# Seeds and table copies of an S4D kernel generator moved in the planned order of a two-head kernel

## The chip, the cores and the metric

One core of a Trainium2 chip runs the whole kernel in one launch. The metric is the device time of that core in microseconds (us). The number to predict is the median of several runs of the changed kernel; the kernel before has a median of 586.85 us over 3 runs (586.58 to 588.71). A difference under 0.5% (2.9 us) is about what a measurement of this kernel can't tell from no change.

## The reference

Two heads work on inputs of 2048 positions and 512 channels, and their outputs stand side by side. Head A is a Fourier mix by dense matrices; head B is a long convolution whose kernel comes from a diagonal state-space model with 128 states per channel.

```
a = einsum("bsd,ed->bse", x, dft_hid_re);  b = einsum("bsd,ed->bse", x, dft_hid_im)
yA = einsum("ts,bse->bte", dft_seq_re, a) - einsum("ts,bse->bte", dft_seq_im, b)

A = -exp(log_A_real) + 1j * A_imag;  dt = exp(log_dt);  C = (C_real + 1j * C_imag) * dt[:, None]
P = exp((A * dt[:, None])[:, :, None] * pos[None, None, :])
K = 2.0 * einsum("dn,dnl->dl", C, P).real
yB = irfft(rfft(u, 2L) * rfft(K, 2L), 2L)[:, :, :L] + u * D_skip
out = concatenate([yA, yB], axis=-1)
```

## The kernel before, in words

**The plan.** Every piece of work is a Python generator that yields an engine, an assumed duration, and where it matters an urgency, and then records its instructions. `Plan.run` picks, of all pieces that wait, the one with the earliest start by the assumed durations; a tie is broken by the urgency (lower goes first), then by the number of the piece. So the assumed durations (`act`, `dve`, `load`, the numbers after `yield "pe"`) and the urgencies fix one order of instructions on each engine at build time. On the chip every engine takes its instructions in that order and waits on semaphores.

```
start = max(p[0], self.free.get(engine, 0.0))
...
return start, urgency[0]() if urgency and urgency[0] else p[1], p[2]
```

**Head A (`Fnet`).** There are 8 groups of 16 items and then 4 groups of 8. An item is a 128x512 block of the moving matrix: it is loaded (`raw`, L300, four buffers), split by ScalarE into `hi` (L212) and by VectorE into `lo` (L216) (three pairs of buffers, `DEPTH`), and used by 12 matmuls of 128x512 (L333): four column blocks by three products of high and low parts. The blocks of x (`x_hi`, `x_lo`, same lines) are split once, at the start. There are 1920 matmuls at L333. They are the filling between everything else on TensorE. A group ends in four evacuations `y` (L359).

**Head B (`Ssm`).** The 512 channels are cut into 16 units of 32. For each unit:
- `seed_args` makes angles on ScalarE (L620, four of L622), reduces them on VectorE (L624, L626, L628), and takes Abs, Exp and Sin on ScalarE (L630 to L638, with two ACT_TABLE_LOADs, in front of L632 and L634; for the first unit only the one in front of L634). From the fifth unit on its parameters come by a DMA first (`par`, L568, one buffer).
- `seeds` multiplies them (VectorE, `cs` L647) and copies each half with its sign (ScalarE, L652).
- `tables2` starts the table `t2` (64 powers; one buffer, `t2s`) with copies on ScalarE (L715, L718) and fills it by products (L577), additions (L586, L600, L606) on VectorE and squares (L593) on ScalarE. `tables1` does so for `t1` (32 powers, two buffers; its copy is L695).
- `taps` takes t1 and t2 on TensorE (L773, 128 small matmuls); only then is `t2` free for the next unit.

Two units make one `stage1_k` (L803). Beside it run the spectrum of u (L848, 8 times, at the start), 16 products of spectra (L929 on TensorE, then `uk` L941 on ScalarE, which frees the PSUM bank, then VectorE L944 to L957), their inverse (L964, joined to the next `taps` where one is left) and 8 last steps (L1011). All small TensorE work of head B shares two pairs of PSUM banks (`fs`).

## Time and profile before

| what | value |
|---|---|
| median of 3 runs | 586.85 us |
| the profiled execution, its own time | 587.23 us |
| its span, first to last instruction | 585.4 us |
| TensorE busy | 578.6 us (99%) |
| VectorE busy | 494.8 us (85%) |
| ScalarE busy | 381.4 us (65%) |

A matmul is pipelined: it shows 0.39 us, while the next one starts after 0.23 us. "Idle before" in a row is the time in which the engine had nothing to do in front of that instruction, with the one that ended the wait behind the arrow.

### The profile page before, as it was taken

What the parts mean: (1) busy time and instruction counts of PE and PEld (TensorE: products, weight loads), DVE (VectorE), ACT (ScalarE), POOL (GpSimd) and SP (SyncE); (2) the same over time, 40 slices, a digit from 0 to 9 for tenths busy, and PEclk for the clock granted to TensorE, in tenths of its full rate; (3) what the DMA queues carried; (4) which work ended last, traced back from release to release, by engine and by line L of the source; (5) the groups of instructions that cost most, each with busy time, mean ns of one, the idle gap of its engine ahead of it and who ended that gap; (6) DMA issues with size and microseconds to landing.
All of it is one profiled execution on the core that took longest, in us unless ns stands there. A gap on an engine that the chain in (4) does not pass through costs nothing.

```text
span 585.4 us, 14916 instructions
## 1 busy us (share of the span) xinstructions
PE 578.6 (99%) x5968; PEld 441.6 (75%) x5968; DVE 494.8 (85%) x883; ACT 381.4 (65%) x745; POOL 4.0 (1%) x12
## 2 busy tenths in 40 slices
PE   8999999999999999999999999999999999999997
PEld 7767677788777877787777778777877777777775
DVE  6986989999999999999999999999999984252620
ACT  4789894954775668677775777596756535354622
POOL 0000000000000000000000000000000000000000
PEclk9999999999999999999999999999999999999999
DMA  8999996473384276735987685458698945899684
GB/s 262 324 356 333 309 331 217 125 204 107 103 264 119 87 194 187 208 90 145 273 241 214 170 255 147 134 154 270 194 296 235 266 128 176 219 354 301 200 260 145
DMA packets 141238, 125.84 MB, mean 215 GB/s; under 512 B 46192, under 2 KB 106352, under 8 KB 140912
## 3 DMA queue, kind: packets, MB, share of 16 engines
q1 hardware_dynamic: 140880, 124.48, 70.1%
q8 instruction: 47, 0.77, 0.6%
q10 hardware_dynamic: 288, 0.39, 0.2%
q14 instruction: 23, 0.19, 0.1%
HBM read 82.12 MB, written 42.73 MB: 213 GB/s over the span
## 4 chain that ended last, share of the span: by engine, by line
PE 92%; ACT 3%; DMA 2%; DVE 1%; issue 1%; SPq 0%; DVEq 0%; ACTq 0%
PE acc L333 72%; PE f L773 5%; PE f L929 5%; PE f L964 3%; PE f L848 3%; PE f L1011 3%; PE f L803 2%; DMA par<-par_dram 1%; DMA raw<-in_sT 1%; ACT hi L212 1%; ACT L634 0%; DVE prod L577 0%; ACT seed L622 0%; ACT xk_sb L812 0%; ACT y L359 0%
## 5 line engine op out<-in xcount | busy, mean ns | idle before, releaser
L333 PE MATMUL acc<-hi,x_hi 128*128 128x512 f32 x640 | 257.0, 402 | 0.6 <-ACT x_hi L212 0.5
L333 PE MATMUL acc<-lo,x_hi 128*128 128x512 f32 x640 | 249.9, 390 | 0.0
L333 PE MATMUL acc<-hi,x_lo 128*128 128x512 f32 x640 | 249.5, 390 | 0.0
L577 DVE TENSOR_TENSOR prod<-t,cs 128x1024 f32<-128x1024 f32 (+4 forms) x192 | 163.9, 870 | 3.3 <-ACT t L715 1.3
L333 PEld LDWEIGHTS acc<-hi,x_hi 128*128 128x128 f32 x640 | 120.1, 188 | 48.0 <-issue 20.8
L216 DVE TENSOR_TENSOR lo<-raw,hi 128x512 fp32r<-128x512 f32 x160 | 109.9, 687 | 52.9 <-ACT hi L212 39.4
L212 ACT ACTIVATE hi<-raw 128x512 fp32r<-128x512 f32 x160 | 100.7, 630 | 80.5 <-PE acc L333 56.6
L333 PEld LDWEIGHTS acc<-hi,x_lo 128*128 128x128 f32 x640 | 120.3, 188 | 26.4 <-DVE x_lo L216 0.5
L333 PEld LDWEIGHTS acc<-lo,x_hi 128*128 128x128 f32 x640 | 120.2, 188 | 23.2 <-DVE lo L216 0.2
L586 DVE TENSOR_TENSOR t<-prod 128x512 f32<-128x512 f32 (+4 forms) x192 | 95.1, 514 | 1.1
L593 ACT ACTIVATE square<-t 128x256 f32<-128x256 f32 (+1 forms) x64 | 36.7, 573 | 26.3 <-DVE t L586 25.0
L941 ACT ACTIVATE uk<-f 128x1024 f32<-128x1024 f32 x32 | 31.6, 1015 | 5.5 <-PE f L929 4.8
L773 PEld LDWEIGHTS f<-t,t 128*32 128x32 f32 x2048 | 29.4, 110 | 7.5 <-issue 4.1
L359 ACT ACTIVATE y<-acc 128x512 f32<-128x512 f32 x47 | 27.8, 597 | 11.0 <-PE acc L333 10.8
L773 PE MATMUL f<-t,t 128*32 128x64 f32 x2048 | 32.1, 220 | 1.4 <-ACT uk L941 1.4
L929 PE MATMUL f<-xt,w 64*32 64x256 f32 x1024 | 31.3, 379 | 0.1
L944 DVE TENSOR_TENSOR z<-uk 128x512 f32<-128x512 f32 x32 | 22.0, 687 | 9.8 <-ACT uk L941 9.8
L929 PEld LDWEIGHTS f<-xt,w 64*32 64x32 f32 x1024 | 18.6, 106 | 10.8 <-issue 4.3
L606 DVE TENSOR_TENSOR t<-square 128x128 f32<-128x128 f32 (+1 forms) x64 | 24.8, 388 | 0.0
L979 ACT ACTIVATE z<-f 128x512 f32<-128x512 f32 x32 | 17.4, 597 | 11.1 <-PE f L773 7.2
L652 ACT ACTIVATE cs<-cs 128x352 f32<-128x352 f32 x32 | 15.8, 541 | 13.3 <-DVE cs L647 13.3
L600 DVE SCALAR_TENSOR_TENSOR t<-t 128x128 f32<-128x128 f32 (+2 forms) x48 | 22.4, 466 | 0.2
(81 smaller groups left out, 409.7 us busy)
## 6 DMA issues: line engine op xcount, KB each, us to landing
raw<-in_sT SPq DMA_DIRECT2D x127, 256.0 KB, 3.7
p<-y SPq DMA_DIRECT2D x32, 256.0 KB, 3.4
xt<-xu SPq DMA_DIRECT2D x32, 256.0 KB, 4.6
xk<-xk_sb SPq DMA_DIRECT2D x32, 256.0 KB, 4.0
xt<-xk SPq DMA_DIRECT2D x32, 256.0 KB, 5.1
zs<-z SPq DMA_DIRECT2D x32, 256.0 KB, 4.0
zl<-zs SPq DMA_DIRECT2D x16, 512.0 KB, 6.2
raw<-p SPq DMA_DIRECT2D x32, 256.0 KB, 4.2
```

The lines of the kernel that those rows point to most:

```text
L212: self.nc.scalar.activation(hi, src, AF.Copy)
L216: self.nc.vector.tensor_tensor(lo, src, hi.bitcast(F32), op=OP.subtract)
L333: nc.tensor.matmul(acc[d], l[:, cols], r, start=k == 0 and n == 0, stop=k == len(items) - 1 and n == 2)
L359: self.nc.scalar.activation(y, ps, AF.Copy, scale=-1.0 if g[2] == 1 else 1.0)
L577: self.nc.vector.tensor_tensor(p.rearrange("p k d c m -> p k (d c) m"), src.rearrange("p d c l -> p (d c) l")[:, None, :, rows].to_broadca ...
L586: self.nc.vector.tensor_tensor(dst[:, :, :, rows], p[:, 0], p[:, 1, :, ::-1], op=OP.add)
L593: self.nc.scalar.activation(sq, t[:, :, :, m // 2:m], AF.Square)
L600: self.nc.vector.scalar_tensor_tensor(t[:, :, 1, m:2 * m:2], t[:, :, 0, m // 2:m], 2.0, t[:, :, 1, m // 2:m], op0=OP.mult, op1=OP.mult)
L606: self.nc.vector.tensor_tensor(t[:, :, 0, m:2 * m:2], box[0][:, :, 0], box[0][:, :, 1], op=OP.subtract)
L773: nc.tensor.matmul(ps[32 * j:32 * j + 32, i], t1[:, d, c], t2[:, d, c], start=c == 0, stop=c == 1, tile_position=(0, 32 * j))
L929: nc.tensor.matmul(both[:, :, c], self.w2[rows, 2 * q + r, xx, 32 * c:32 * c + 32], xt[rows, r, xx], start=True, stop=True, tile_position= ...
L941: a.activation(uk[:, r].rearrange("p g n c d -> p g (n c d)"), p, AF.Copy)
```

## The change

No instruction is added or taken away; only urgencies and assumed durations change, so the order changes. The first unit's `seed_args` gets urgency -1 in place of 1, those of later units 1.8 in place of 1. `cs` (L647, L652) and the copies into the tables (L695, L715, L718) get the new urgency `soon` (-1). The assumed time of the first item's DMA, which ScalarE issues, falls from 0.78 + 3.3 us to 2.6 us; five assumed ScalarE durations rise; a joined `taps` is taken as 1.78 + 1.1 us in place of 1.78 + 0.87; the fetch of TensorE's next instructions is taken to be asked for 3.6 us behind the point at which it falls due, not 3.0.

```
-ASKED, APART_BY, COMES = 3.0, 4.3, 2.4
+ASKED, APART_BY, COMES = 3.6, 4.3, 2.4
+def soon():
+    return -1
...
             yield "act", 0.45
             self.nc.scalar.dma_start(raw, src)
-            yield "dma2", load(256)
+            yield "queue", 2.6
...
-        yield "act", act(2 * n) + 4 * act(0)
+        yield "act", 1.7
         a.activation(args[:, :, 0], par[:, 0:2], AF.Copy)
...
-        yield "act", act(n)
+        yield "act", 0.5
         a.activation(k, r, AF.Abs)
-        yield "act", act(n) + 1.3
+        yield "act", 0.5 + 1.3
         a.activation(e, e, AF.Exp, scale=-1.0)
...
-        yield "dve", dve(22 * CHUNK)
+        yield "dve", dve(22 * CHUNK), soon
         self.nc.vector.tensor_tensor(cs[:, :, :, :, 0], s[:, 1:3], s[:, 0:1].to_broadcast([128, 2, 11, CHUNK]),
...
-            yield "act", act(11 * CHUNK)
+            yield "act", 0.5, soon
             self.nc.scalar.activation(cs[:, n, :, :, 1], cs[:, n, :, :, 0], AF.Copy, scale=sign)
...
-        self.plan.spawn(self.seed_args(0, *args[0]), 1)
+        self.plan.spawn(self.seed_args(0, *args[0]), -1)
...
-                self.plan.spawn(self.seed_args(n + 1, *args[n + 1]), 1)
+                self.plan.spawn(self.seed_args(n + 1, *args[n + 1]), 1.8)
...
-            yield "act", act(2 * CHUNK)
+            yield "act", act(2 * CHUNK), soon
             a.activation(t[:, :, :, 1].rearrange("p d c -> p c d"), cs[:, :, 0, :, 0], AF.Copy)
...
-        yield "pe", 1.78 + (0.87 if other else 0), None, 322 if other else 257
+        yield "pe", 1.78 + (1.1 if other else 0), None, 322 if other else 257
```

The changed file is five lines longer ahead of all this work, so L212 of before is L217 of after, and so on.

**Place 1, the start on ScalarE.** The first item (`hi`, `raw`) and the first two blocks of x (`x_hi_146` in two pieces, then `x_hi_153`). Before:

```order
L296 DMA raw<-in_sT 128x512
L250 ACT_TABLE_LOAD
L250 ACTIVATE x_hi_146<-uk 128x128
L212 ACTIVATE hi<-raw 128x512
L212 ACTIVATE x_hi_153<-uk 128x512
L212 ACTIVATE x_hi_146<-uk 128x384
```

After:

```order
L301 DMA raw<-in_sT 128x512
L217 ACT_TABLE_LOAD
L217 ACTIVATE hi<-raw 128x512
L255 ACTIVATE x_hi_146<-uk 128x128
L217 ACTIVATE x_hi_146<-uk 128x384
L217 ACTIVATE x_hi_153<-uk 128x512
```

The first item's split moved ahead of the first piece of x, and the rest of x's first block ahead of its second block. VectorE's `lo` and `x_lo` follow in the same order.

**Place 2, the first unit's seeds on ScalarE** (`seed`, the lines from Abs to the last Sin; `zl` is an evacuation of the spectrum of u). Before:

```order
L630 ACTIVATE seed<-seed 128x352
L632 ACTIVATE seed<-seed 128x352
L634 ACT_TABLE_LOAD
L634 ACTIVATE seed<-seed 128x192
L212 ACTIVATE hi<-raw 128x512
L212 ACTIVATE x_hi_390<-uk 128x512
L858 ACTIVATE zl<-f_376 128x512 x2
L858 ACTIVATE zl<-f_377 128x512
L212 ACTIVATE x_hi_414<-uk 128x512
L212 ACTIVATE x_hi_431<-uk 128x512
L212 ACTIVATE hi<-raw 128x512
L212 ACTIVATE x_hi_442<-uk 128x512
```

After:

```order
L635 ACTIVATE seed<-seed 128x352
L637 ACTIVATE seed<-seed 128x352
L639 ACT_TABLE_LOAD
L639 ACTIVATE seed<-seed 128x192
L641 ACTIVATE seed<-seed 128x160
L643 ACTIVATE seed<-seed,halfpi 128x352
L217 ACTIVATE hi<-raw 128x512 x2
L217 ACTIVATE x_hi_381<-uk 128x512
L657 ACTIVATE cs<-cs 128x352 x2
L217 ACTIVATE hi<-raw 128x512
L720 ACTIVATE t_126<-cs 128x2x32
L723 ACTIVATE t_126<-cs 128x2x32 x2
```

Before, ten other instructions stand between the first Sin and the two last of the seeds; after, none, and the copies of `cs` and into the tables follow in the six rows behind them.

**Place 3, VectorE where the first tables begin** (`t_126` is t2, `t_625` and `t_484` are t1). Before:

```order
L626 TENSOR_TENSOR seed<-seed 128x352
L628 TENSOR_SCALAR seed<-seed 128x352
L216 TENSOR_TENSOR lo<-raw,hi 128x512 x3
L647 TENSOR_TENSOR cs<-seed 128x704
L577 TENSOR_TENSOR prod_638<-t_126,cs 128x128
L577 TENSOR_TENSOR prod<-t_625,cs 128x128
L586 TENSOR_TENSOR t_126<-prod_638 128x64
```

After:

```order
L629 TENSOR_SCALAR seed<-seed 128x352
L582 TENSOR_TENSOR prod_502<-t_126,cs 128x128
L631 TENSOR_TENSOR seed<-seed 128x352
L591 TENSOR_TENSOR t_126<-prod_502 128x64
L582 TENSOR_TENSOR prod<-t_484,cs 128x128
L633 TENSOR_SCALAR seed<-seed 128x352
L582 TENSOR_TENSOR prod_584<-t_126,cs 128x384
```

Before, the second unit's seed steps, three `lo` and the second unit's `cs` stand ahead of the first product; after, the first products stand between the second unit's seed steps, and no `lo` among them.

**Counted over the whole order.** TensorE has the same 137 runs of work in both orders, with 63 runs of L333 in each; what changes is how many matmuls of L333 lie in them. Ahead of the thirteenth `taps` stand 1338 matmuls of L333 before and 1266 after, and in both the same small pieces (12 of L773, 8 each of L848, L929 and L964, 6 of L803, 2 of L1011). Ahead of the fourteenth it is 1440 and 3 of L1011 before, 1395 and 4 after. Ahead of the first `taps` stand 273 and 7 runs of L848 before, 261 and 5 after. On VectorE, up to the last addition into the tables of the thirteenth unit, stand 687 instructions before and 677 after: six `lo` fewer, and one each fewer of L577 128x512, L577 128x256, L586 128x64x4 and L586 128x64x2. In VectorE's order 127 instructions before and 110 after read what the one right ahead of them wrote. On SyncE's queue the first three constants (0.25 MB) move from place 12 behind the loads of x to place 32, and w2 with ia (1 MB) from place 70 to place 40. On ScalarE, between the seventh unit's L620 and the first `uk` stand three `y`, three `hi` and two squares before, three `hi` and two squares after. ACT_TABLE_LOADs are 32 in both; GpSimd's order is the same.

## Rows read from the trace of the kernel before

**Rows 1.** The page, part 1: busy time of each engine

```profile
PE 578.6 (99%) x5968; PEld 441.6 (75%) x5968; DVE 494.8 (85%) x883; ACT 381.4 (65%) x745; POOL 4.0 (1%) x12
```

**Rows 2.** Waits of TensorE: line, waited for, total us, times, longest

```profile
PE f L773 <- ACT uk L941: 1.4, 1, 1.4
...
PE acc L333 <- ACT x_hi L212: 0.5, 1, 0.5
```

**Rows 3.** Timeline, 127 to 145 us, TensorE: start, us, instruction, count, idle

```profile
127.18 0.39 PE L333 MATMUL acc<-hi,x_hi 128*128 128x512 f32 x1
...
144.63 0.39 PE L333 MATMUL acc<-hi,x_lo 128*128 128x512 f32 x1
```

**Rows 4.** Timeline of the first 9 us, the three engines

```profile
3.56 0.31 ACT L250 ACTIVATE x_hi<-uk 128x128 fp32r<-128x128 f32 x1 [1.10 <-DMA uk<-in_x]
3.82 0.63 ACT L212 ACTIVATE hi<-raw 128x512 fp32r<-128x512 f32 x1
5.38 1.04 ACT L212 ACTIVATE x_hi<-uk 128x512 fp32r<-128x512 f32 x2 [0.93 <-DMA uk<-in_x]
6.04 1.16 DVE L216 TENSOR_TENSOR x_lo<-uk,x_hi 128x512 fp32r<-128x512 f32 x2 [0.87 <-ACT x_hi L212]
6.48 0.50 PE L333 MATMUL acc<-hi,x_hi 128*128 128x512 f32 x1 [0.48 <-ACT x_hi L212]
7.26 0.50 PE L333 MATMUL acc<-hi,x_lo 128*128 128x512 f32 x1
```

**Rows 5.** Timeline, 165 to 179 us: ScalarE, then TensorE

```profile
165.61 0.26 ACT L620 ACTIVATE seed<-par 128x64 f32<-128x64 f32 x1 [2.05 <-DMA par<-par_dram]
...
172.44 0.50 ACT L632 ACTIVATE seed<-seed 128x352 f32<-128x352 f32 x1
172.95 1.28 ACT L634 ACT_TABLE_LOAD   x1
174.25 0.37 ACT L634 ACTIVATE seed<-seed 128x192 f32<-128x192 f32 x1
...
175.74 1.00 ACT L941 ACTIVATE uk<-f 128x1024 f32<-128x1024 f32 x1
...
176.80 1.99 PE L773 MATMUL f<-t,t 128*32 128x64 f32 x128 [1.40 <-ACT uk L941]
```

**Rows 6.** Stretches: length, busy us of PE, PEld, DVE, ACT, POOL, clock, DMA

```profile
0.00:39.40 39.40, 37.72 (x160) 28.69 (x161) 33.53 (x74) 25.75 (x48) 0.20 (x4) 1.00 0.90 308
39.40:51.50 12.10, 12.10 (x53) 8.17 (x53) 4.77 (x9) 11.95 (x28) 0.00 (x0) 1.00 0.96 343
51.50:101.00 49.50, 49.50 (x332) 35.65 (x328) 47.36 (x89) 39.22 (x82) 0.00 (x0) 1.00 0.85 288
101.00:397.00 296.00, 294.53 (x3342) 228.71 (x3341) 290.83 (x519) 207.12 (x417) 3.11 (x6) 1.00 0.61 173
```

**Rows 7.** Timeline, 47 to 87 us, VectorE

```profile
47.46 0.69 DVE L216 TENSOR_TENSOR lo<-raw,hi 128x512 fp32r<-128x512 f32 x1 [4.42 <-ACT hi L212]
...
83.15 1.23 DVE L577 TENSOR_TENSOR prod<-t,cs 128x1024 f32<-128x1024 f32 x1
84.41 0.69 DVE L586 TENSOR_TENSOR t<-prod 128x512 f32<-128x512 f32 x1
86.80 0.69 DVE L216 TENSOR_TENSOR lo<-raw,hi 128x512 fp32r<-128x512 f32 x1 [1.69 <-ACT hi L212]
```

**Rows 8.** Timeline, 393 to 399 us: VectorE, then TensorE

```profile
393.28 1.22 DVE L577 TENSOR_TENSOR prod<-t,cs 128x1024 f32<-128x1024 f32 x1
394.41 0.69 DVE L216 TENSOR_TENSOR lo<-raw,hi 128x512 fp32r<-128x512 f32 x1
395.01 0.42 DVE L606 TENSOR_TENSOR t<-square 128x256 f32<-128x256 f32 x1
395.35 0.69 DVE L586 TENSOR_TENSOR t<-prod 128x512 f32<-128x512 f32 x1
...
397.23 1.99 PE L773 MATMUL f<-t,t 128*32 128x64 f32 x128
```

More of the change, by code (lines that the diff above doesn't have):

```diff
@@ L636, in seed_args @@
         a.activation(r[:, 6:11], r[:, 6:11], AF.Sin, scale=-TWO_PI)
-        yield "act", act(n)
+        yield "act", 0.5
         a.activation(k, k, AF.Sin, scale=-TWO_PI, bias=self.halfpi)
@@ L713, in tables2 @@
             cs, t = self.cs[n], self.t2
-            yield "act", act(2 * CHUNK)
+            yield "act", act(2 * CHUNK), soon
             a.activation(t[:, :, :, 1].rearrange("p d c -> p c d"), cs[:, :, 0, :, 0], AF.Copy)
             for c in range(2):
-                yield "act", act(2 * CHUNK)
+                yield "act", act(2 * CHUNK), soon
                 a.activation(t[:, :, c, 2:6:2].rearrange("p d j -> p j d"), cs[:, c, 1:3, :, 0], AF.Copy)
```

## The prediction

> **What bounds the kernel now.** I read the page's busy times first. TensorE is busy for 578.6 of 585.4 us [rows 1], so what is left to win is what TensorE waits for, and the reader should see how little that is. The waits of TensorE name one wait in the middle, 1.4 us in front of a `taps` (L773), and 0.5 us at the start [rows 2]. Everything else is the beat of the matmuls: from the first row to the last of [rows 3] there are 77 steps in 17.45 us, 0.227 us each. The small pieces of head B and the switches to and from them cost their time too, but the change touches neither: both orders have 137 runs of work, 63 of them of L333, so no switch is saved. The tables' engine is VectorE. Its idle time by stretches [rows 6] is 39.4 - 33.5 = 5.9 us at the start, 12.1 - 4.8 = 7.3 us from 39.4 to 51.5 us, 2.1 us up to 101 us, and 5.2 us in the 296 us up to 397 us: 20.5 us before the thirteenth unit's tables are ready. After 51.5 us it is nearly never idle. So there are two tracks. TensorE reaches a `taps` when the matmuls ahead of it are done, VectorE when the tables are done, and the later one sets the time.
>
> **The start (place 1).** Before, ScalarE splits the first piece of x at 3.56 us and the first item right behind it at 3.82 us [rows 4], so the item's load had landed by 3.82 us. Then it waits until 5.38 us for x's second block, with the rest of the first block behind it in the queue, although that load was issued earlier. VectorE's two `x_lo` start at 6.04 us, and TensorE goes on at 6.48 us, after 0.48 us of idling, and reaches the next step that needs an `x_lo` only at 7.26 us [rows 4]. After the change the item goes first: at most 3.82 + 0.63 us, then 0.31 us for the piece, so the first matmul comes some 0.2 us later. That is made good, since the rest of the first block now stands ahead of the second block. It can start at about 4.7 us (both ahead of it done) and at the latest at 5.38 us. With 0.5 us on ScalarE and 0.6 us on VectorE its low part is there between 5.9 and 6.6 us, in place of 7.2 us (6.04 + 1.16). TensorE then runs through two steps from about 6.1 us. I take 0.7 us gained; the ends are 0.4 and 0.9 us, and a loss is not in sight, because every load keeps its place.
>
> **The wait at 176.8 us.** Before, the seventh unit's seeds stand ahead of the two `uk` on ScalarE. Their parameters came late (2.05 us of idling in front of L620 at 165.61 us), then came the steps with two table loads, and `uk` started only at 175.74 us; it holds the PSUM bank that the `taps` wants, which began at 176.80 us after 1.40 us of idling [rows 5]. Between that L620 and the first `uk` stand three `y`, three `hi` and two squares before; after, three `hi` and two squares, and the first `y` only behind the first `uk` (the later units' seeds and the product are no longer of one urgency). Three `y` at about half a microsecond each are the 1.4 us. I take the 1.4 us as gone; the other end is that it stays.
>
> On this chain a table load shows 1.28 us, it begins 0.01 us after the step ahead of it has ended and the next step begins 0.02 us behind it [rows 5]. The Trainium skill, "ScalarE: Activation LUTs", section "What ACT_TABLE_LOAD costs", counts 1283 ns and a drain of about 1380 ns more for each switch; the load agrees with the row, no drain shows in it. By that page the first unit's seeds would be 1.4 us longer, and the sum would be 0 to 1.4 us higher; I go by the row.
>
> **VectorE's tables against TensorE (places 2 and 3).** This is the term that decides. The thirteenth `taps` now has 1338 - 1266 = 72 matmuls fewer ahead of it and the same small pieces: TensorE is there 72 x 0.227 = 16.3 us earlier, and by 0.7 + 1.4 us more for the two gains above. It began at 397.23 us [rows 8], so without any wait it would begin at 397.2 - 18.4 = 378.8 us. VectorE finished these tables at 395.35 + 0.69 = 396.04 us [rows 8]. It has ten instructions fewer ahead: six `lo` at 0.60 us from start to start (394.41 to 395.01 in [rows 8]), and four of the table steps, together about 1.5 us: 5.1 us. An instruction that reads what the one right ahead wrote starts 1.26 us behind a product of 128x1024 (83.15 to 84.41 us) [rows 7], any other 1.13 us (393.28 to 394.41 us) [rows 8]; 17 such neighbours fewer are up to 2.2 us (0 at the other end; I take 2.2). With the old idle time the tables would be ready at 396.0 - 5.1 - 2.2 = 388.7 us. So VectorE has to lose 388.7 - 378.8 = 9.9 us of its 20.5 us of idle time, or TensorE waits.
>
> What goes: the idle 7.3 us from 39.4 to 51.5 us [rows 6]. The longest part is 4.42 us in front of a `lo` at 47.46 us [rows 7], which stood behind the second unit's seeds on ScalarE, while the first unit's `cs` copies were not done and VectorE had no table to work on. With the first unit's seeds in one piece (place 2) and products between the second unit's seed steps (place 3) there is work. Also 0.87 us at the start [rows 4] and 1.69 us at 86.80 us [rows 7]. What comes: I laid the new order of the first three units end to end with the durations above. It leaves about 1.0 us in front of the third unit's seed steps, behind ScalarE, and about 2.5 us in front of the fourth unit's, since the single `t2` is not free until the first `taps` is done. Both are estimates; I take 3.5 us. Net 0.9 + 7.3 + 1.7 - 3.5 = 6.4 us, so 3.5 us are missing. They have to come out of the 5.2 us of idling after 101 us [rows 6]. If half of these go, because the table copies and `cs` now are first on ScalarE, 3.5 - 2.6 = 0.9 us of waiting is left for TensorE; if all go, none; if none, 3.5 us. I take 0.9 us. Ahead of the fourteenth `taps` the lead is only 45 matmuls less one L1011 (10.2 - 2.1 = 8 us), so from there on TensorE is again the later one.
>
> **At no cost.** The new durations and the 2.6 us only move places in the plan. On SyncE's queue 1 MB of w2 comes earlier, into a stretch where the DMA engines are 90% busy [rows 6]; the cover is that an item lasts 12 x 0.227 = 2.7 us on TensorE, which never waited for a load there [rows 2]; without cover 1 MB at the 308 GB/s of that stretch is 3.4 us. The first constants come later, but the first L848 too. GpSimd's queue is as before.
>
> **Sum.** 585.4 - 0.7 - 1.4 + 0.9 = 584.2 us of span. The profiled execution took 587.23 us, 1.8 us more than its span, and 0.4 us above the median; so 584.2 + 1.8 - 0.4 = about 585.7 us in the median.
>
> **Rivals.** *Nothing waits.* All of VectorE's later idle time that is missing goes: 585.4 - 0.9 - 1.4 = 583.1 us of span, 584.5 us. For it speaks that before the change no `taps` waited for VectorE at all [rows 2]; against it that TensorE is now asked to be there 16 us earlier and VectorE is full after 51.5 us. This is also the floor: more than 2.3 us isn't there to win, so a gain over 0.5% (2.9 us) needs luck.
>
> *It does not do what it says.* The new waits take what the start and the `taps` gave: 3.5 us of waits in place of 0.9, or the 1.4 us stay: 586 to 588 us, about 587.
>
> *Slower.* The seeds of later units stand behind other work now (1.8 in place of 1), with table loads in their chain. If one unit's seeds come as late as the second unit's did before, its step on VectorE holds that in-order queue, its `lo` included, as the 4.42 us at 47.46 us show [rows 7]; tables that have no reserve pass it to TensorE in full. Then 0.9 + 4.4 = 5.3 us of waits: 585.4 - 2.1 + 5.3 = 588.6 us of span, 590.0 us; two of them, 594.5 us. It decides from one such wait on, and shows only where VectorE is just in time. Against it: in 296 us before the change such waits made 5.2 us in all [rows 6].
>
> **How the numbers follow.** Forecast 0.60, nothing waits 0.15, does not do what it says 0.13, slower 0.12. The range takes in the floor of 584.5 us with 0.3 us for the spread of runs, 584.2 us, and at the upper end 3.5 us of waits with the lesser gains and no gain at 176.8 us, 585.4 - 0.4 + 3.5 = 588.5 us of span, about 589.9 us; I cut it at 589.2 us. A difference under 0.5% (583.9 to 589.8 us) is no change that can be measured here. Faster by more than that 0.05 (out of the case without waits, by its spread), slower 0.12, no change 0.83.
>
> **What would show it.** In the changed profile the second block of matmuls should start near 6.1 us; VectorE should be idle for under 3 us between 39 and 52 us; first products on VectorE before 42 us; the first `taps` near 75.5 us, the thirteenth near 379 to 380 us; ScalarE free for `uk` before the fifth `taps`. Waits of TensorE on L586 or L577 in front of L773 of 0 to 3.5 us in all are this term. It is wrong if TensorE waits elsewhere (for `hi`, a bank, a load), or if these waits pass 5 us.

## The result, and the profile after

The changed kernel takes 589.58 us in the median of 21 runs (586.89 to 591.24), the kernel before 586.58 us in 21 runs of the same chip (585.8 to 588.71). The ratio is 1.0044, with a 95% interval of 1.0034 to 1.0054: 2.6 us slower by the ratio and 3.0 us by the two medians, where about 1 us faster was forecast. The difference is still under the 0.5% named ahead, but the time lies outside the range, and on the other side. The runs of the changed kernel spread over 4.4 us, those of the kernel before over 2.9 us; that spread turned out to be the trail. One run below, the one that e13's trace comes from, is disturbed (719.31 us, granted clock 0.851); its trace is not read and its time is left out.

The profiled execution took 590.08 us, its span is 588.3 us. First the page of the changed kernel, part 1 (busy time) and the first line of part 4 (the chain that ended last, by engine). All lines of the changed kernel have numbers 5 higher than before (L333 is L338, L773 is L778, L941 is L946).

```profile
PE 582.2 (99%) x5968; PEld 443.7 (75%) x5968; DVE 492.9 (84%) x883; ACT 380.6 (65%) x745; POOL 4.9 (1%) x12
...
PE 60%; DVE 30%; issue 5%; DMA 2%; ACT 2%; SPq 0%; DVEq 0%; ACTq 0%
```

The same 5968 matmuls keep TensorE busy for 3.6 us longer than in [rows 1]. A matmul counts as busy for as long as it runs, so this is the first hint at slower matmuls and not at waits. In the chain VectorE now holds 30% (1% before).

The waits of TensorE (answering [rows 2]; line, waited for, total us, times, longest):

```profile
PE acc L237 <- DVE y L211: 1.1, 1, 1.1
PE f L778 <- issue: 0.6, 1, 0.6
PE acc L338 <- ACT x_hi L255: 0.3, 1, 0.3
PE acc L338 <- ACT y L364: 0.2, 1, 0.2
PE acc L338 <- DVE lo L221: 0.2, 1, 0.2
```

The 1.4 us for `uk` are gone; the first line, in front of the empty matmuls that warm TensorE up (L237), stood there before too. No wait stands in front of a `taps` for its table. What is new is small and in three places, and "issue" (nothing that the profile shows) stands inside a `taps`.

The start (timeline, TensorE, changed kernel; start us, duration, instruction, idle before), answering the TensorE rows of [rows 4]:

```profile
4.67 0.79 PE L338 MATMUL acc<-hi,x_hi 128*128 128x512 f32 x1 [0.25 <-ACT x_hi L255]
5.40 0.80 PE L338 MATMUL acc<-hi,x_lo 128*128 128x512 f32 x1
5.99 0.63 PE L338 MATMUL acc<-lo,x_hi 128*128 128x512 f32 x1
...
7.27 0.63 PE L338 MATMUL acc<-lo,x_hi 128*128 128x512 f32 x1
7.70 0.63 PE L338 MATMUL acc<-hi,x_lo 128*128 128x512 f32 x1
...
9.83 0.63 PE L338 MATMUL acc<-lo,x_hi 128*128 128x512 f32 x1
...
10.57 0.40 PE L338 MATMUL acc<-hi,x_hi 128*128 128x512 f32 x1
10.80 0.40 PE L338 MATMUL acc<-lo,x_hi 128*128 128x512 f32 x1
```

The first two matmuls of x before, which stand ahead of those in [rows 4]:

```profile
4.50 0.80 PE L333 MATMUL acc<-hi,x_hi 128*128 128x512 f32 x1
5.10 0.45 PE L333 MATMUL acc<-hi,x_lo 128*128 128x512 f32 x1
```

In the changed kernel nothing is waited for from 7.27 us on, and yet a matmul comes every 0.43 us up to 10.26 us, and from 10.57 us on every 0.23 us. That is TensorE at 1.2 and at 2.4 GHz. The trace's record of the granted clock says the same: full from 10.43 us here, from 5.19 us in the kernel before. (The page and the view by stretches show 1.00 in both, also for the first microseconds; the pace of equal matmuls is the surer sign.)

Where the 2.9 us between the two profiled spans are (585.4 and 588.3 us), from the starts of all blocks of matmuls, each against the least time that such a block takes (in the third row some 1.8 us are the three stretches, the rest is small pieces):

| place | before | changed | difference |
|---|---|---|---|
| start, up to the steady beat | 5.3 us | 6.9 us | +1.6 us |
| in front of the fifth `taps` | 1.5 us | 0 | -1.5 us |
| waits at 282 to 292, 336 to 357 and 391 to 401 us, and a few of 0.1 us | 0 | 2.0 us | +2.0 us |
| stall inside the fifteenth `taps` (L778) | 0 | 0.8 us | +0.8 us |
| all blocks, to the start of the last matmul | 581.3 us | 584.2 us | +2.9 us |

The stretches of [rows 6] after the change (length, busy us of PE, PEld, DVE, ACT, POOL, clock, DMA):

```profile
0.00:39.40 39.40, 38.09 (x155) 31.35 (x156) 31.79 (x71) 25.34 (x53) 0.20 (x4) 1.00 0.87 289
39.40:51.50 12.10, 12.10 (x53) 8.68 (x51) 12.04 (x29) 8.88 (x16) 0.00 (x0) 1.00 0.88 316
51.50:101.00 49.50, 49.50 (x393) 32.92 (x396) 45.74 (x77) 43.98 (x93) 0.00 (x0) 1.00 0.86 293
101.00:397.00 296.00, 295.55 (x3464) 228.12 (x3454) 294.00 (x529) 208.57 (x422) 4.17 (x6) 1.00 0.61 179
```

VectorE's 7.3 us of idling from 39.4 to 51.5 us have become 0.06 us, as foreseen, and the 5.2 us after 101 us have become 2.0 us. In all 13.4 us are left of 20.5 us.

### The profile page after: what moved, and what is told of

Same layout as the page of the kernel before. It is cut to its first block, busy times and chain, and to the rows that moved or that the text cites. A ratio compares the mean times of both kernels' runs of the same rounds, so it can differ in the third digit from the quotient of the medians.

```text
span 588.3 us, 14931 instructions
## 1 busy us (share of the span) xinstructions
PE 582.2 (99%) x5968; PEld 443.7 (75%) x5968; DVE 492.9 (84%) x883; ACT 380.6 (65%) x745; POOL 4.9 (1%) x12
## 4 chain that ended last, share of the span: by engine, by line
PE 60%; DVE 30%; issue 5%; DMA 2%; ACT 2%; SPq 0%; DVEq 0%; ACTq 0%
PE acc L338 47%; DVE prod L582 10%; DVE t L591 6%; DVE lo L221 6%; PE f L934 3%; PE f L778 3%; PE f L853 3%; PE f L1016 2%; PE f L969 2%; PE f L808 1%; DVE t L611 1%; DVE z L949 1%; DVE cs L652 1%; DMA raw<-in_sT 1%; DMA xt<-xk 1%
## 5 line engine op out<-in xcount | busy, mean ns | idle before, releaser
L338 PE MATMUL acc<-hi,x_hi 128*128 128x512 f32 x640 | 258.0, 403 | 0.5 <-ACT x_hi L255 0.3
L338 PE MATMUL acc<-lo,x_hi 128*128 128x512 f32 x640 | 251.2, 393 | 0.2 <-DVE lo L221 0.2
L338 PE MATMUL acc<-hi,x_lo 128*128 128x512 f32 x640 | 250.3, 391 | 0.0
L338 PEld LDWEIGHTS acc<-hi,x_hi 128*128 128x128 f32 x640 | 120.6, 188 | 48.8 <-issue 21.6
L217 ACT ACTIVATE hi<-raw 128x512 fp32r<-128x512 f32 x160 | 100.6, 628 | 83.2 <-PE acc L338 71.2
L338 PEld LDWEIGHTS acc<-hi,x_lo 128*128 128x128 f32 x640 | 120.7, 189 | 26.6 <-DVE x_lo L257 0.4
L338 PEld LDWEIGHTS acc<-lo,x_hi 128*128 128x128 f32 x640 | 120.8, 189 | 24.2 <-DVE lo L221 1.2
L364 ACT ACTIVATE y<-acc 128x512 f32<-128x512 f32 x47 | 27.7, 595 | 13.4 <-PE acc L338 13.0
L946 ACT ACTIVATE uk<-f 128x1024 f32<-128x1024 f32 x32 | 31.8, 1016 | 6.2 <-PE f L934 3.9
L778 PEld LDWEIGHTS f<-t,t 128*32 128x32 f32 x2048 | 29.5, 110 | 6.8 <-issue 4.9
L778 PE MATMUL f<-t,t 128*32 128x64 f32 x2048 | 32.2, 220 | 0.6 <-issue 0.6
L934 PE MATMUL f<-xt,w 64*32 64x256 f32 x1024 | 31.3, 379 | 0.0
L934 PEld LDWEIGHTS f<-xt,w 64*32 64x32 f32 x1024 | 18.4, 106 | 10.9 <-issue 3.5
L951 DVE TENSOR_TENSOR uk<-uk 128x512 f32<-128x512 f32 x32 | 22.1, 690 | 0.7
```

The lines of the kernel that those rows point to most:

```text
L217: self.nc.scalar.activation(hi, src, AF.Copy)
L338: nc.tensor.matmul(acc[d], l[:, cols], r, start=k == 0 and n == 0, stop=k == len(items) - 1 and n == 2)
L364: self.nc.scalar.activation(y, ps, AF.Copy, scale=-1.0 if g[2] == 1 else 1.0)
L778: nc.tensor.matmul(ps[32 * j:32 * j + 32, i], t1[:, d, c], t2[:, d, c], start=c == 0, stop=c == 1, tile_position=(0, 32 * j))
L934: nc.tensor.matmul(both[:, :, c], self.w2[rows, 2 * q + r, xx, 32 * c:32 * c + 32], xt[rows, r, xx], start=True, stop=True, tile_position= ...
L946: a.activation(uk[:, r].rearrange("p g n c d -> p g (n c d)"), p, AF.Copy)
```

## The experiments

Each run has its own median of the kernel before, from the same chip (586.5 to 587.2 us); ratios are against that. "61st" is the start of the 61st matmul of x, when every kernel runs at its beat; before the change it is 19.86 us.

**Is it the clock, or the order of the data?** e1 and e2 change only the number of the empty warm-up matmuls ahead of x, in the changed kernel and in the kernel before; the order of everything else stays.

```diff
-        self.zeros(7)
+        self.zeros(10)     # e1, in the changed kernel
-        self.zeros(7)
+        self.zeros(5)      # e2, in the kernel before
```

> The changed kernel with ten pairs of warm-up matmuls in place of seven; the order of all other matmuls is as in the changed kernel. Theory (granted clock): the changed kernel loses 1.6 us at the start because TensorE idles between the end of the warm-up and the first matmuls of x, and the granted clock stays at 0.5 until 10.43 us in place of 5.19 us. With more warm-up it should rise near 5.2 us, the first matmul of x comes at about 5.4 us, and the time falls from 589.6 to about 587.9 us. Rival (order of the data): the start is late because x's pieces are split in another order; then the longer warm-up only delays the first matmul by 0.7 us and the time is 589.6 to 590.3 us.

> The kernel before with five pairs of warm-up matmuls in place of seven; the order of all other matmuls is as in the kernel before. Theory (granted clock): about 0.9 us more idling of TensorE ahead of the first matmul of x makes the granted clock rise later than 5.19 us, near 10 us, and the time grows by 1 to 2 us, to 587.6 to 588.6 us. Rival (order of the data): nothing waits for the warm-up matmuls; the time stays at 586.6 us within 0.3 us.

Measured: e1 587.41 us, ratio 1.0008 [0.9995, 1.0020], runs within 1.9 us; full clock from 5.75 us, 61st at 19.49 us. e2 588.17 us, ratio 1.0020 [1.0008, 1.0032]; 1.05 us of idling ahead of the first matmul of x, full clock from 7.43 us. Work that nobody needs made the changed kernel 2.2 us faster. Laid side by side, e1's trace gains 2.0 us on the first one at the start, and 0.9 us because a stall inside the fifteenth `taps` (below) is missing. The order of the data at the start can't be what costs by itself: e1 has the changed order.

e2 came out as expected, but not for the reason expected. Its 61st matmul starts at 19.89 us, that of the kernel before at 19.86 us, so the later rise cost it nothing there. Its profiled run took 589.05 us, the longest of twelve, and what makes its span 1.9 us longer are new stalls inside the seventh and the ninth `taps` (0.73 and 0.56 us between two matmuls; the seventh below) and 0.6 us of waiting for a `zl` load:

```profile
232.87 1.87 PE L778 MATMUL f<-t,t 128*32 128x64 f32 x117
235.25 0.41 PE L778 MATMUL f<-t,t 128*32 128x64 f32 x11 [0.51 <-issue]
```

So e2 speaks neither for the clock nor against it.

**The start alone, and all but the start.** e3 gives the kernel before the one edit that puts the item ahead of x's first piece; e4 takes it out of the changed kernel. Both plan the later work anew.

```diff
-            yield "dma2", load(256)
+            yield "queue", 2.6     # e3, in the kernel before; e4 is the reverse in the changed one
```

> The kernel before with the part of the change at the start alone: the first item's load is planned at 2.6 us, so ScalarE splits it ahead of x's first piece. The later order moves too (the first taps has 252 matmuls ahead of it in place of 273). Theory (granted clock): the start loses 1.6 us as in the changed kernel, granted clock up near 10.4 us, time 588 to 589 us if the rest costs nothing new. The prediction's step: gain of 0.7 us at the start, about 585.9 us.

> The changed kernel with the start as in the kernel before (x's first piece split ahead of the item), all else of the change kept; the later order moves too (the first taps has 240 matmuls ahead of it, the thirteenth 1278). Theory (granted clock): granted clock up at 5.2 us, start 1.6 us earlier, about 588 us if the waits of the later stretches stay as in the changed kernel, 585 to 586 us if they go. Rival (order of the data): the 0.7 us the prediction gave the start are lost, 590.3 us.

Measured: e3 588.17 us, ratio 1.0021 [1.0004, 1.0039], with runs from 586.5 to 590.7 us; e4 587.46 us, ratio 1.0009 [0.9996, 1.0021], runs within 1.9 us. e4's trace has full clock from 4.84 us and none of the new waits for `y` or `lo`, and yet e4 is not at the 585 to 586 us expected for that case: its 61st matmul comes at 20.17 us, after 0.7 us of waiting for x's second block, and 0.5 us is waited for a `zl` load. The median of e3 is as the clock theory has it, but its trace, of a 586.7 us run, shows full clock from 4.59 us, that is during the gap ahead of x, and a start 0.5 us better than before. So one order of the start has a good and a bad outcome, and the trace had caught the good one. That asked for more traces of one kernel.

**The same kernel, several traces.** e7, e10 and e11 are the changed kernel as it is, e12 the kernel before.

> The changed kernel once more, for a second trace. Theory (granted clock differs from run to run): the rise lies anywhere from 4.6 to 10.5 us and the span follows it; the 60th matmul of x comes between 19.5 and 21.6 us. The stall of 0.9 us inside the fifteenth taps, which no wait explains, should not come back at that place. The waits at 282 to 291, 334 and 390 us, 1.6 us together, should come back, since they follow from the order. Rival (all of it is the order): the same rise near 10.4 us and the same stall.

> The changed kernel a third time. Theory (the rise of the granted clock differs from run to run and sets the time): span = 585.8 us for a rise near 5.5 us and 588.3 us for one near 10.4 us; a rise in between gives a span in between. The stall in the fifteenth taps (0.85 and 0.9 us in the two traces so far) comes again, since it now looks tied to the place in the instruction stream. Rival: a span that does not follow the rise.

> As e10, a fourth trace of the changed kernel: the later the granted clock rises, the longer the span, between 585.8 and 588.5 us or more; the stall in the fifteenth taps again.

> The kernel before a second time (with five empty lines, so that its line numbers are those of the changed kernel). Theory: here the rise seldom comes late; it lies between 4.3 and 7.5 us, the span between 584.8 and 586 us; the 1.4 us in front of the fifth taps come again. Rival: a rise near 10 us as often as in the changed kernel, span 587 to 588 us.

| trace | idle ahead of x's first matmul | full granted clock from | 61st | span |
|---|---|---|---|---|
| changed, profiled | 0.25 us | 10.43 us | 21.50 us | 588.3 us |
| changed, e7 | 0.23 us | 5.52 us | 19.18 us | 585.8 us |
| changed, e10 | 0.56 us | 9.83 us | 21.38 us | 589.7 us |
| changed, e11 | 0.34 us | 9.26 us | 21.01 us | 587.8 us |
| before, profiled | 0.1 us, not listed | 5.19 us | 19.86 us | 585.4 us |
| before, e12 | 0.1 us, not listed | 4.16 us | 19.48 us | 584.3 us |

This is the timeline of e7's TensorE at the start, to be laid beside the one above:

```profile
4.64 0.80 PE L338 MATMUL acc<-hi,x_hi 128*128 128x512 f32 x1 [0.23 <-ACT x_hi L255]
5.37 0.55 PE L338 MATMUL acc<-hi,x_lo 128*128 128x512 f32 x1
5.76 0.39 PE L338 MATMUL acc<-lo,x_hi 128*128 128x512 f32 x1
...
6.13 0.48 PE L338 MATMUL acc<-hi,x_hi 128*128 128x512 f32 x1
6.44 0.40 PE L338 MATMUL acc<-lo,x_hi 128*128 128x512 f32 x1
6.67 0.40 PE L338 MATMUL acc<-hi,x_lo 128*128 128x512 f32 x1
```

The data is ready at the same times as in the first trace; only the clock rose in time, and the second step starts at 6.13 us and the 61st matmul 2.3 us earlier than in the first trace. Against the kernel before it is 0.68 us earlier by its profiled run and 0.30 us by e12. Three of four traces of the changed kernel have the late rise, none of the two of the kernel before. The Trainium skill, "TensorE: Matmul & The Clock Gate", Part 1, "What you observe", says that the transition to the fast matmuls varies by half a microsecond either way from run to run; here it lies from 5.52 to 10.43 us in four runs of one program.

The idling alone doesn't decide: e3 idled 0.50 us there and had full clock from 4.59 us, e4 0.22 us and 4.84 us, e2 1.05 us and 7.43 us. Only traces with 0.25 to 0.56 us of idling show a rise after 9 us, but not all of these do.

The rise alone doesn't order the spans either: e10 has the longest span with the second latest rise, since TensorE also waits 1.8 us for `zl` loads there (e11 0.8 us for `xt`; neither trace of the kernel before has a listed wait for a load). And my first expectation for the stall in the fifteenth `taps`, that it would not come back, was wrong: the longest step between two of its matmuls is 0.83 us in the profiled run, 0.78 us in e7 and 0.76 us in e10; only in e11 it is 0.09 us. Nor did the 1.4 us in front of the fifth `taps` come again in e12 (ScalarE, then TensorE, beside [rows 5]):

```profile
164.27 0.26 ACT L625 ACTIVATE seed<-par 128x64 f32<-128x64 f32 x1 [1.09 <-DMA par<-par_dram]
...
175.46 1.99 PE L778 MATMUL f<-t,t 128*32 128x64 f32 x128 [0.56 <-ACT uk L946]
```

**Covering the gap more closely, and elsewhere.** e5 is e3 and e6 the kernel before, both with ten pairs; e16 is the changed kernel with eight.

```diff
-        self.zeros(7)
+        self.zeros(10)     # e5, in the kernel of e3; e6, in the kernel before
-        self.zeros(7)
+        self.zeros(8)      # e16, in the changed kernel
```

> The kernel of e3 (before, with the item ahead of x's first piece) with ten pairs of warm-up matmuls in place of seven, its order otherwise as in e3. Theory (granted clock): e3's twelve runs spread over 4.2 us (586.5 to 590.7) because the time at which the granted clock rises differs from run to run, and its gap ahead of the first matmul of x decides whether the rise comes before or after; without the gap the median falls from 588.2 to about 586.5 us and the runs lie within about 2 us of each other. Rival (the spread is of the later stretches): median and spread as in e3.

> The kernel before with ten pairs of warm-up matmuls in place of seven, its order otherwise unchanged. Theory (granted clock): the gap ahead of the first matmul of x is 0.3 us in the kernel before, which seldom costs anything, and what waits for the second block of x at 6.48 us stays: 586.3 to 586.8 us, no change against 586.7 us. Rival (the warm-up only delays the first matmuls of x by 0.7 us): 587.0 to 587.5 us.

> The changed kernel with eight pairs of warm-up matmuls in place of seven: the warm-up ends at about 4.8 us, where the first item and x's first piece are just ready. Theory (the gap decides when the granted clock rises): the rise lies between 4.2 and 7.5 us, the median falls from 589.6 to 587.3 to 588.2 us (the stall in the fifteenth taps may stay), and the runs spread over about 2 us. Rival (three pairs in e1 helped through something else, such as the place of the code): 589 us or more, spread of 4 us as in the changed kernel.

Measured: e5 588.54 us, ratio 1.0039 [1.0026, 1.0052]; e6 586.82 us, ratio 1.0010 [1.0000, 1.0021]; e16 588.45 us, ratio 1.0027 [1.0016, 1.0039]. e16's runs lie within 1.1 us of each other (588.07 to 589.2) where the changed kernel's lie within 4.4 us: with one pair more the late rises seem to be gone, and with them about 1 us of the median. In its one trace the gap isn't closed (0.27 us of idling are left), but the full clock came at 3.88 us, inside the longer warm-up, and the 61st at 19.18 us; the stall grew to 1.49 us, which may be why the median stays above the expectation. In the eight traces with ten pairs that are read here, in whatever order (e1, e5, e6, e8, e9, e14, e15, e17), the full clock comes at 4.28 to 7.24 us, never later. More warm-up has a price too: with ten pairs x's first matmul comes at 5.34 us in most of them, and in the traces of e5 and e6, where the rise came at 7.2 us, the 61st comes at 20.16 us. e5 missed its expectation by 2 us. Its spread shrank as expected (2 us over six runs, in place of 4.2 over twelve), but its trace shows 1.06 us of stall inside the ninth `taps` and 0.5 us of waits for `zl`; e3's, of its second fastest run, shows 1.27 us of that stall and no wait for `zl`.

**The stall inside a `taps`.** TensorE in the changed kernel, then in e1, e16 and e18 (below); four timelines in turn:

```profile
451.04 1.75 PE L778 MATMUL f<-t,t 128*32 128x64 f32 x107
453.40 0.53 PE L778 MATMUL f<-t,t 128*32 128x64 f32 x21 [0.61 <-issue]
```

```profile
448.84 1.99 PE L778 MATMUL f<-t,t 128*32 128x64 f32 x128
```

```profile
449.48 1.70 PE L778 MATMUL f<-t,t 128*32 128x64 f32 x105
452.45 0.54 PE L778 MATMUL f<-t,t 128*32 128x64 f32 x23 [1.27 <-issue]
```

```profile
283.00 1.81 PE L778 MATMUL f<-t,t 128*32 128x64 f32 x113
286.94 0.43 PE L778 MATMUL f<-t,t 128*32 128x64 f32 x15 [2.13 <-issue]
```

128 matmuls go in 1.92 us, one in 15 ns, or they stop after 105 to 117. Where they stop is a fixed place in the program: after 107 in all traces of the changed kernel, after 105 with two warm-up matmuls more (e16); after 115 in e3 and 109 with six more (e5); after 113 in the seventh `taps` of the kernel before and 117 with four fewer (e2). What arrives there is code. The DMA part of the profile has a queue of kind "instruction": 47 packets of 16 KB in the whole span, and one of them falls exactly here (the changed kernel, 450.5 to 453.5 us; packets, MB, share):

```profile
q8 instruction: 1, 0.02, 2.6%
```

Set beside the start of the packet in the trace, the stall (the longest step between two matmuls of the `taps`) follows it:

| trace, `taps` | packet, against the start of the `taps` | stall |
|---|---|---|
| e1, fifteenth | 2.5 us ahead | none |
| e11, fifteenth | 1.0 us ahead | 0.09 us |
| before, seventh | 0.6 us ahead | 0.14 us |
| changed, fifteenth | 0.2 us ahead | 0.83 us |
| e2, ninth | 0.2 us ahead | 0.56 us |
| e2, seventh | at the start | 0.73 us |
| e10, fifteenth | at the start | 0.76 us |
| e5, ninth | 0.4 us behind | 1.06 us |
| e3, ninth | 0.6 us behind | 1.27 us |
| e16, fifteenth | 0.6 us behind | 1.49 us |
| e18, ninth | 1.5 us behind | 2.35 us |

Wherever it stalls, TensorE goes on 2.2 to 2.6 us behind the packet's start. The Trainium skill, "Runtime: NRT & Kernel Launch", "Instruction fetch mechanics", describes this queue (blocks of 16 KiB, fetched by the engine's own sequencer) and calls the cost of crossing a block "mostly hidden". Here it is hidden behind the large matmuls, and not where 128 small ones eat 256 instructions in 1.92 us. What sets the packet's place I can't say: e1 differs from the changed kernel by six matmuls at the start, and its packet came 2.3 us sooner against the `taps`, while two matmuls more (e16) made it come 0.8 us later. The kernel's planner has a guess at it (`Plan.fetched`, which the edit of `ASKED` moves), and it did not keep these packets clear of the `taps`. e8, with the old `ASKED`, shows no such stall, but its order and its warm-up differ too, so whether this edit brings the stall is not shown.

**The waits at 280 to 400 us.** In the changed kernel they show on `y` and on `lo` (timeline of TensorE, beginnings of the waits):

```profile
287.49 0.50 PE L338 MATMUL acc<-hi,x_hi 128*128 128x512 f32 x1 [0.22 <-ACT y L364]
...
350.75 0.50 PE L338 MATMUL acc<-lo,x_hi 128*128 128x512 f32 x1 [0.19 <-DVE lo L221]
```

and on ScalarE, just ahead of them, squares of the tables wait for VectorE with `y` and `uk` queued behind (changed kernel, ScalarE):

```profile
283.94 0.42 ACT L598 ACTIVATE square<-t 128x256 f32<-128x256 f32 x1 [2.28 <-DVE t L591]
284.27 0.58 ACT L364 ACTIVATE y<-acc 128x512 f32<-128x512 f32 x1
285.41 0.63 ACT L598 ACTIVATE square<-t 128x512 f32<-128x512 f32 x1 [0.56 <-DVE t L591]
285.95 1.01 ACT L946 ACTIVATE uk<-f 128x1024 f32<-128x1024 f32 x1
286.85 0.58 ACT L364 ACTIVATE y<-acc 128x512 f32<-128x512 f32 x1
```

My first theory was that ScalarE is to blame, since the plan hands it the squares too early now (the five assumed durations that changed there rose). e8 puts the old durations back (`ASKED`, the seeds' times on ScalarE, the paired `taps`); e9 and e13 keep the order of all instructions and cut the tie between squares and VectorE, e9 in one direction, e13 and e17 (the same kernel) in both; the squares read a constant there, so the right doubling of the tables is left out. All have the ten pairs of e1, so e1's 587.41 us is what they stand against.

```diff
-ASKED, APART_BY, COMES = 3.6, 4.3, 2.4
+ASKED, APART_BY, COMES = 3.0, 4.3, 2.4                                    # e8
-        yield "act", 1.7
+        yield "act", act(2 * n) + 4 * act(0)                              # e8, and L634, L636, L642
-        yield "pe", 1.78 + (1.1 if other else 0), None, 322 if other else 257
+        yield "pe", 1.78 + (0.87 if other else 0), None, 322 if other else 257   # e8
-        self.nc.scalar.activation(sq, t[:, :, :, m // 2:m], AF.Square)
+        self.nc.scalar.activation(sq..., self.halfpi.to_broadcast([128, d * m]), AF.Square)   # e9, e13, e17
-        ... tensor_tensor(t[:, :, 0, m:2 * m:2], box[0][:, :, 0], box[0][:, :, 1], ...)
+        ... tensor_tensor(t[:, :, 0, m:2 * m:2], t[:, :, 0, m // 2:m], t[:, :, 1, m // 2:m], ...)   # e13, e17
```

> The changed kernel with ten pairs of warm-up matmuls (587.4 us) and with the planner's old durations for the seeds, the packets and the paired taps; urgencies and the start as changed. The order of the tables moves with it. Theory (the squares of ScalarE stand too early in its queue because the plan now holds ScalarE for faster than VectorE can follow): the waits of TensorE behind y and lo in 280 to 395 us, 1.6 us, go, the time is 585.8 to 586.5 us. Rival (they come from the urgencies): waits of 1 to 2 us stay, 587 to 588 us, here or at other places.

> The changed kernel with the longer warm-up (e1, 587.4 us), in which the squares of the tables (L598) read a constant in place of the table's rows: same instructions in the same order on every engine, but ScalarE no longer waits for VectorE in front of a square. The imaginary rows' doubling is therefore computed from wrong squares; the time of each instruction is unchanged. Theory (the new waits of TensorE come from ScalarE's queue, where a square that waits 2.3 to 2.7 us for VectorE holds back y and uk): the 0.84 us at 280 us and the 0.21 us at 389 us go, the 0.5 us at 334 us (behind a lo) stays or falls; 586.2 to 586.5 us. Rival (TensorE waits there for banks that VectorE's z or a DMA holds): the waits stay, 587.2 to 587.6 us.

> As e9, and VectorE's step that used a square (L611) reads the table itself in place of the square, so no square waits for VectorE and VectorE waits for no square; the results of the doubling are wrong, the instructions and their order are as in e1. Theory (ScalarE's waits for VectorE hold back y and uk): the waits of TensorE at 280 us (0.84 us) and 389 us (0.2 us) go, 586.2 to 586.6 us. Rival (ScalarE has too much queued there, whether it waits or not: square, uk, y, hi, y, hi, uk in 5 us): they stay at 0.5 us or more, 587 to 587.5 us.

> The kernel of e13 again, for a trace that can be read. Theory (ScalarE's waits for VectorE hold back y and uk): no idling of ScalarE in front of the squares at 281 to 285 us and no waits of TensorE at 280 and 389 us. Rival (too much stands in ScalarE's queue there): ScalarE busy without a break and TensorE's 0.84 us stay at 0.5 us or more. e13's median, 587.8 us, already speaks for the rival.

Measured: e8 587.25 us, ratio 1.0011 [1.0000, 1.0022]; its waits for `y` and `lo` are gone, with 2.3 us lost at other places in its trace (1.1 us of it in waits for `zl` loads); e9 587.23 us, ratio 1.0012 [0.9999, 1.0025]; e13 587.70 us, ratio 1.0013 [1.0000, 1.0026]; e17 one run of 587.93 us. None is measurably faster than e1. The theory falls, and e17 shows what stands behind it. Its ScalarE no longer waits in front of a square (the third `y` comes at 283.17 us, in e1 at 284.81 us), and TensorE waits just as long, now for VectorE (e17: VectorE, then TensorE):

```profile
284.85 0.42 DVE L605 SCALAR_TENSOR_TENSOR t<-t 128x256 f32<-128x256 f32 x1
285.19 0.42 DVE L611 TENSOR_TENSOR t<-t 128x256 f32<-128x256 f32 x1
285.52 0.69 DVE L591 TENSOR_TENSOR t<-prod 128x512 f32<-128x512 f32 x1
286.12 0.69 DVE L949 TENSOR_TENSOR z<-uk 128x512 f32<-128x512 f32 x1
286.73 0.69 DVE L221 TENSOR_TENSOR lo<-raw,hi 128x512 fp32r<-128x512 f32 x1
```

```profile
286.50 0.39 PE L338 MATMUL acc<-hi,x_hi 128*128 128x512 f32 x1
287.47 0.50 PE L338 MATMUL acc<-lo,x_hi 128*128 128x512 f32 x1 [0.58 <-DVE lo L221]
```

The whole loss of that stretch is 0.84 us in e1, 0.83 us in e9 and 0.84 us in e17. VectorE is idle for 0.03 to 0.07 us of the ten from 278 to 288 us, in these three and in the changed kernel; the `lo` that TensorE needs stands behind table steps in its queue. Take ScalarE's delay away, and VectorE's is as long.

**Which part of the change brings them?** e14 is e1 with the later units' seeds back at urgency 1, e15 is e1 with the table copies and `cs` back at their usual urgency (and the copies of `cs` at their old assumed duration).

```diff
-                self.plan.spawn(self.seed_args(n + 1, *args[n + 1]), 1.8)
+                self.plan.spawn(self.seed_args(n + 1, *args[n + 1]), 1)       # e14
-        yield "act", act(2 * CHUNK), soon
+        yield "act", act(2 * CHUNK)                                           # e15, and L651, L656, L699, L722
```

> e1 (587.4 us) with the later units' seeds back at urgency 1 in place of 1.8. Theory (the seeds that stand behind other work bring the waits, through the lo and y queued with them): the waits of TensorE at 280 to 390 us fall from 1.6 us to under 0.5 us, unless the wait for uk in front of a taps (1.4 us in the kernel before) comes back; 586 to 587.4 us. Rival (the table copies' urgency brings them): 1 us or more stays.

> e1 (587.4 us) with the table copies and the cs products back at the usual urgency in place of -1. Theory (copies ahead of everything push y, hi and uk back on ScalarE): the waits of TensorE at 280 to 390 us fall under 0.5 us, 586 to 586.6 us if no taps waits for its table instead. Rival (the seeds' urgency brings them): 1 us or more stays; or first products come later and a taps waits for VectorE, 587.5 us or more.

Measured: e14 589.62 us, ratio 1.0050 [1.0036, 1.0064]; e15 589.37 us, ratio 1.0036 [1.0023, 1.0048]. Both theories fall again, to the other side: without either part it is 2 us worse. The waits of TensorE in e14 (e15 has 1.5 us for `lo` and 0.5 us for a `zl` load):

```profile
PE acc L338 <- DVE lo L221: 2.0, 2, 1.2
```

So neither part alone brings the waits; in this order each pays off in the presence of the other. Nor do the two together always bring them: e4 and e8 have both parts, and no wait for `y` or `lo` in their traces, but waits for `zl` loads. Which wait an order ends with is not a matter of one urgency.

**One part alone, with one pair of warm-up more.**

```diff
-        self.plan.spawn(self.seed_args(0, *args[0]), 1)
+        self.plan.spawn(self.seed_args(0, *args[0]), -1)     # e18, in the kernel before, with zeros(8)
```

> The kernel before with the first unit's seeds at urgency -1 (one line of the change) and eight pairs of warm-up matmuls. Its tables are ordered as in e3, which had neither the 1.4 us in front of the fifth taps nor the 1.6 us at 280 to 390 us but a stall of 1.3 us inside the ninth taps. Theory (the first unit alone is worth its 1.4 us): 585.3 to 586 us if no stall falls into a taps, 586.5 us with one. Rival (each new order finds its own wait): 586.5 to 588 us.

Measured: e18 588.13 us, ratio 1.0025 [1.0009, 1.0041]. Neither the wait for `uk` nor the waits at 280 us are in its trace, but 2.35 us of stall are, inside the ninth `taps` (last fence on the stall, above). No version tried beats the kernel before.

## Why the prediction was wrong

The steps in its own order.

*What bounds the kernel.* Right: TensorE at its beat, the same number of runs of work, 1.4 us of waiting in front of one `taps`.

*The start.* This is the step that failed: "a loss is not in sight, because every load keeps its place". The order came as foreseen, and with the clock up in time (e7) the gain is 0.68 us, where 0.7 us was forecast; that so little is missing is partly luck, since against e12, in which x's second block came sooner, it is 0.30 us. But the step counted the matmuls of the first 10 us by the beat of [rows 3], which belongs to the fast clock. In [rows 4] the matmuls of the first step (the first one slow, 0.80 us) were not shown, and I never asked at which level TensorE stood there. The 0.2 us by which the first matmul comes later, written down as "made good", fell where the warm-up had just ended, and in three of four traces the full clock then came at 9.3 to 10.4 us. In the profiled run this is 1.6 us lost, 2.3 us from the forecast, and e7, the same program with the clock up in time, has these 2.3 us back. That the late rise is what was lost is shown by that; that the gap behind the warm-up brings it is argued, and e3 and e4 show that it need not. In the medians, more warm-up gave back 1 us with one pair (e16, with a longer stall) and 2.2 us with three (e1, without the stall).

*The wait at 176.8 us.* It is gone as forecast: `uk` is through long before the fifth `taps` (changed kernel, ScalarE and TensorE; compare [rows 5]):

```profile
155.62 0.24 ACT L625 ACTIVATE seed<-par 128x64 f32<-128x64 f32 x1
...
163.72 1.28 ACT L639 ACT_TABLE_LOAD   x1
...
166.52 1.00 ACT L946 ACTIVATE uk<-f 128x1024 f32<-128x1024 f32 x1
...
169.37 1.99 PE L778 MATMUL f<-t,t 128*32 128x64 f32 x128
```

The reason given for it did not hold. No `y` stands between the seeds' first step and the first `uk` now, and yet from the one to the other it takes 10.9 us, where it took 10.1 us before. What changed is the start of the seeds: 10.1 us ahead of the end of the product's matmuls (L929, now L934), before only 4.0 us, in part because the parameters are there in time. In the kernel before the wait for `uk` follows the wait for `par`: 1.40 and 2.05 us in the profiled run, 1.12 and 1.79 us in e2, 0.96 and 1.49 us in e6, 0.56 and 1.09 us in e12. So 1.4 us was also the largest of four, and the size was in part luck; and with the later seeds back at the old urgency (e14) the wait does not come back.

*VectorE's tables against TensorE.* The account of VectorE's idle time was right, and its end was mis-sized and misplaced. VectorE lost 7.1 us of idling before 397 us; the first `taps` came at 77.85 us and the thirteenth at 382.5 us, late against 75.5 and 379 to 380 us by the 2.3 us of the start, and the second by 1.5 us of the new waits too. First products run from 42.88 us, 0.9 us later than I said. No `taps` waits for its table. But VectorE is as full as feared, and what is late for it is a `lo` in its own queue, and a `y` on ScalarE behind squares that wait for VectorE: up to 2.0 us in place of 0.9, mostly in three places that the forecast covered with "It is wrong if TensorE waits elsewhere".

*At no cost.* Wrong in one point: a new order also moves the place in the code at which a block of instructions has to be fetched. The stall of 0.8 us inside the fifteenth `taps` is a term that the sum did not have. The loads cost nothing in the profiled run, as said; in two of the other three traces of the changed kernel they did (1.8 us for `zl` in e10, 0.8 us for `xt` in e11).

*The sum.* Forecast -0.7 - 1.4 + 0.9 = -1.2 us of span; found +1.6 - 1.5 + 2.0 + 0.8 = +2.9 us. With the start covered (e1) the change as a whole stands at 1.0008 against the kernel before, and the kernel before with the same cover (e6) at 1.0010: with the longer warm-up in both, the change gains and loses nothing that can be measured.

*The rivals.* The slower one gave 590.0 us, near what was measured, and that is luck, for its mechanism isn't there: no seed step held the queue for 4.4 us (the longest wait of VectorE for one is 2.1 us), and putting the seeds back made it worse (e14). "It does not do what it says" came nearest in kind: new waits took what the `taps` gave.

What stays open: how often the late rise comes (three of four traces, one of which is the profiled run, and the spread of 21 runs), what decides between an early and a late one, and what decides where a packet of code falls.

## What to carry to other kernels

In the first ten microseconds, see at which pace equal matmuls run before pricing anything there; here a full clock that came about 5 us late cost about 2 us, and three pairs of empty matmuls too many cost nothing that could be measured (e6). When a queue is as full as VectorE's here, moving work up in it makes something else in it late, so price the whole queue and not the wait that has a name. After any reordering look for "issue" inside dense blocks of small matmuls. And read the trace of a run that came out as expected, too: e2 did, for a reason of its own.

## What was not expected of the hardware

- The granted clock of one and the same program rose at 5.52, 9.26, 9.83 and 10.43 us, with x's first matmul at 4.64 to 4.97 us; ahead of each late rise TensorE had idled 0.25 to 0.56 us behind its warm-up. In eight traces with ten pairs it rose at 4.28 to 7.24 us.
- A block of code whose packet started less than 0.25 us ahead of 128 matmuls of 15 ns, or behind their start, stopped them for 0.56 to 2.35 us in the eight such cases of the table and in e7, until 2.2 to 2.5 us behind the start of the packet.
